# First cosine layer of a transformer tail: the first matrix product cut in halves of four token tiles, with the odd tile turned

## The chip, the core and the metric

The kernel runs on one core of a Trainium2 chip. The metric is the device time of one execution in microseconds, the median of several. Engines are named as the profile names them: PE (matmul), PEld (its weight loads), DVE (vector engine), ACT (scalar engine), POOL, and SP, which here only issues DMAs.

## What is computed

Random-feature attention, then a dense mixture of four experts, then a layer with a cosine. The reference, cut to what matters here:

```python
x = attn_out                                  # 1152 tokens x 512
out = sum(p[:, e] * (relu(x @ w1[e]) @ w2[e]) for e in range(4))   # w1 512 x 1024
h = out @ w_in                                # w_in 512 x 2048
g = h * np.cos(h)
return g @ w_out                              # w_out 2048 x 512
```

## The kernel before

The 2048 features of the cosine layer are done as two layers of 1024, so that six layers of one shape follow each other: e = 0 to 3 are the experts, e = 4 (E in the code) is the **first cosine layer**, e = 5 the **second cosine layer**. Tokens lie in nine tiles of 128. All matrix products are in float32r with each operand split into a high and a low part, so one product of blocks is three matmuls per 128 of depth.

**First product of a layer** (`first_product`, L552). The 1024 features are cut in four blocks p = 0 to 3 of two times 128. Tokens and weights of a block form a two by two scheme, which a Strassen-Winograd form does with seven products of six matmuls each: a, d, b, c, e are written to a fresh PSUM bank each, a2 is added onto the bank of a, and c2 onto the bank of c (`reopen`). After d, b, c, e and c2 DVE adds the bank into `h` (L571); after a ACT copies it. The token side uses sums T1 to T4 and the weight side sums S (the `load_a` chain: ACT splits at L129, DVE subtracts at L134 and forms sums at L184). c2 can't write its bank before DVE's add of c has read it.

In a layer that is `wide` the two token halves have four tiles (matmuls of 512 columns) and the ninth, the **odd tile**, is done apart by `odd_tile` (L522) with tokens as stationary operand and weights as moving one, so its result is turned and is turned back by eight transposes in the second product (L654). `together` says how many weight blocks one such matmul takes: two (512 columns), or one (256). Before, layers 1 to 3 and 5 are wide, `together` is two in 1 to 3 and one in 5. Layer 4 isn't wide: its halves have three tiles (384 columns), and the three tiles left over are done by `plain` (L509) with 24 matmuls of 384 columns per block.

**Second product** (`Second`, L632). Per token tile 24 matmuls of 512 columns (L704). Ahead of each half tile ACT and DVE split `h` into a high and a low part (`sth`, L674; `stl`, L677 or L282).

**Cosine** (`settle`, L386). A finished piece of `h` goes on `line`, and `from_line` (L429) takes one every `pace` quanta: ACT L400 and L401, DVE L403, ACT L408 (the sine), DVE L410 (the product). The scratch has three buffers. In layer 4 pieces of the last token chunk wait until the second product; in layer 5 pieces of the first token half wait until quantum 30.

**What sets the order.** A quantum is some six or twelve matmuls. `dense` (L839) runs the products, and after each quantum lets the pending helpers take one step; `plan` (L805) says after which quantum of which layer a helper starts. Engines are in order. Weight slots are handed on by `place` and `retired`: a weight load's split is issued once the slot's last reader is. Raw weights pass through two buffers (`new_raw`); the DMAs for them are issued by SP. The turned tokens of layer 4 come from the experts' sum `acc`: `second_x(1)` and `second_sums` in layer 3, `second_x(0)` for tiles 0 to 2 after quantum 2 of layer 4, since these three are the last of layer 3's order. The sums of the first column of tiles are made in layer 4's second product by `token_sums`, for layer 5.

Of the kernel before, what the change touches and what calls it, by code (L numbers as in the profile page):

```python
# [9 lines left out]
F32 = mybir.dt.float32  # L10
# [16 lines left out]
def performer_moe_kernel(ctx, tc, q, k, v, omega, probs, w1, w2, w_in, w_out, out):  # L27
# [59 lines left out]
    def wide(e, p):  # L87
        return 0 < e < E or e == E + 1

    def together(e):  # L90
        return 2 if e < E else 1
# [192 lines left out]
    def sum_out(n, src, cols):  # L284
        return split(nc.vector, src, *sums(n, cols))
# [38 lines left out]
    def token_sums(cols):  # L324
# [15 lines left out]
        ready.add(cols.start)  # L340
# [3 lines left out]
    def second_sums():  # L344

        cols = slice(1, HALF)
        r1, r2 = spare(cols)
        whole(r2, tokens(0, LO, cols))
        low = turn_acc(2, LO)
        yield  # L350
        for (_, tp), z in zip(low, range(J)):
            minus(r1[:, z], as_tiles(tp), r2[:, z])
        high = turn_acc(2, HI)
        yield
        put_second_x(2, high)
        parts = sum_out(1, r1, cols)
        next(parts)
        yield
        yield from parts
        for (_, tp), z in zip(high, range(J)):  # L360
            minus(r1[:, z], as_tiles(tp), r1[:, z])
        yield from wait(2)
        yield from rest_sums(r1, r2, cols)

# [64 lines left out]
    def from_line(q):  # L429

        since[0] += 1
        late_ = q >= FIRST[E]
        ready = sorted(
            (x for x in line if (x[3] > E and (x[0] == 2 or q >= 30)) or (x[3] == E and (x[0] < NCH - 1 or late_))),
            key=lambda x: (x[3], -x[0] if x[3] > E else x[0], *x[1:]),
        )
        pace = 2 if late_ or ready and ready[0][3] > E else 3
        if ready and ready[0][3] > E and ready[0][0] == 2 and ready[0][2] == NPF - 1:
            pace = 1
        if ready and since[0] >= pace:  # L440
            since[0] = 0
            line.remove(ready[0])
            c, i, p, e = ready[0]
            settled(e, c, i, p, None)
# [77 lines left out]
    def odd_tile(e, p):  # L522
# [14 lines left out]
        if together(e) > 1:  # L537
            retired.add(("a", e, p))
# [12 lines left out]

    def first_product(e):  # L552
        for p in range(NPF):
            o = not wide(e, p)
            cols = slice(o, HALF)
            W = (HALF - o) * P
            assert ready >= set(range(o, 2))
            a, s = unit("a", e, p), unit("s", e, p)
            A = {(i, j): (a, (i * KD + j * J) * P) for i in range(2) for j in range(2)}
            S = {n: (s, z * J * P) for n, z in ((1, 3), (2, 0), (3, 2), (4, 1))}  # L560
            b11, b21, b22 = (flat(tokens(*z, cols)) for z in ((0, LO), (0, HI), (1, HI)))
            t_ = {n: flat(sums(n, cols)) for n in (1, 2, 3, 4)}
            h = {(i, k): h_of(e, k + 1, i, p) for i in range(2) for k in range(2)}
            bk = {}

            def fresh(n, *args, W=W):
                bk[n] = bank(f"g1_{e}_{p}{n}")[:, :W]
                products(bk[n], *args)

            def add(dst, x, y):  # L570
                nc.vector.tensor_tensor(out=dst, in0=x, in1=y, op=ALU.add)  # L571

            def pa():
                fresh("a", *A[0, 0], b11)
                nc.scalar.activation(h[0, 0], bk["a"], ACTF.Copy)
                yield

            def pd():
                fresh("d", *S[2], t_[2])
                add(h[1, 0], bk["d"], h[0, 0])  # L580
                yield

            def pb():
                fresh("b", *S[1], t_[1])
                add(h[0, 1], bk["b"], h[1, 0])
                yield

            def pc():
                fresh("c", *S[3], t_[3])
                add(h[1, 1], bk["c"], h[0, 1])  # L590
                settle_later(e, 2, 1, p)
                yield

            def pe():
                fresh("e", *S[4], b22)
                add(h[0, 1], bk["e"], h[0, 1])
                settle_later(e, 2, 0, p)
                yield

            def pa2():  # L600
                products(bk["a"], *A[0, 1], b21, False, reopen=True)
                settle_later(e, 1, 0, p, bk["a"])
                yield

            def pc2():
                products(bk["c"], *A[1, 1], t_[4], False, reopen=True)
                add(h[1, 0], bk["c"], h[1, 0])
                settle_later(e, 1, 1, p)
                yield

            def rest(p):
                return [lambda: odd_tile(e, p + 1 - together(e))] * ((p + 1) % together(e) == 0) if wide(e, p) else [lambda i=i: plain(e, 0, i, p) for i in range(2)]

            z = rest(p)
            if e == 0:
                order = [pa, pd, pb, pc, pe, pa2, pc2]
            elif e == E and p == 0 or e == E - 1 and p == NPF - 1:
                order = [pa, pd, pb, pc, pe, pa2, pc2, *z]
            elif e == E and p == NPF - 1:
# [739 lines left out]
```

## Time and profile before

| | |
|---|---|
| Time, median of 3 runs | 656.94 us (656.5 to 657.05) |
| Profiled execution, its own time | 656.51 us |
| Its span | 654.6 us |
| PE busy | 649.9 us, 99% |
| DVE busy | 498.6 us, 76% |
| ACT busy | 362.7 us, 55% |
| POOL busy | 172.9 us, 26% |

The span runs from the first to the last instruction; 1.9 us of the profiled execution lie around it. A matmul record is longer than the distance to the next matmul, since matmuls are pipelined: distances between starts tell what a matmul costs. Layer 4's first product starts at 460.91 and its second at 508.02; layer 5's at 557.02 and 601.83.

### The profile page before, as it was taken

What the parts mean: (1) busy time and instruction counts of PE and PEld (TensorE: products, weight loads), DVE (VectorE), ACT (ScalarE), POOL (GpSimd) and SP (SyncE); (2) the same over time, 40 slices, a digit from 0 to 9 for tenths busy, and PEclk for the clock granted to TensorE, in tenths of its full rate; (3) what the DMA queues carried; (4) which work ended last, traced back from release to release, by engine and by line L of the source; (5) the groups of instructions that cost most, each with busy time, mean ns of one, the idle gap of its engine ahead of it and who ended that gap; (6) DMA issues with size and microseconds to landing.
All of it is one profiled execution on the core that took longest, in us unless ns stands there. A gap on an engine that the chain in (4) does not pass through costs nothing.

```text
span 654.6 us, 9478 instructions
## 1 busy us (share of the span) xinstructions
PE 649.9 (99%) x3407; PEld 568.7 (87%) x3407; DVE 498.6 (76%) x909; ACT 362.7 (55%) x719; POOL 172.9 (26%) x225
## 2 busy tenths in 40 slices
PE   9999999999999999999999999999999999999997
PEld 8999998998888888888888888888999888888887
DVE  6898749779879777679788588689688677596842
ACT  6887764446544545344544345554476874467821
POOL 8888461204332222333432322320000000000000
PEclk9999999999999999999999999999999999999999
DMA  8753121323344534345534245410810001700111
GB/s 190 217 160 98 34 65 33 97 64 114 136 156 140 199 111 142 117 133 171 181 115 145 106 162 176 145 65 4 318 34 32 1 1 50 273 1 1 49 49 49
DMA packets 55439, 70.93 MB, mean 108 GB/s; under 512 B 15200, under 2 KB 40032, under 8 KB 55392
## 3 DMA queue, kind: packets, MB, share of 16 engines
q1 hardware_dynamic: 46800, 40.92, 20.1%
q0 software_dynamic: 8448, 29.37, 12.9%
q8 instruction: 27, 0.44, 0.3%
q14 instruction: 20, 0.16, 0.1%
q10 hardware_dynamic: 144, 0.03, 0.0%
HBM read 55.36 MB, written 14.94 MB: 107 GB/s over the span
## 4 chain that ended last, share of the span: by engine, by line
PE 99%; DVE 0%; issue 0%
PE g L704 45%; PE g L503 5%; PE g_odd L533 3%; PE g_0a L503 2%; PE g_3a L503 2%; PE g_2c L503 2%; PE g_2a L503 2%; PE g_1a L503 2%; PE g_0c L503 2%; PE g_3c L503 2%; PE g_1c L503 2%; PE kv L1085 2%; PE num L1114 2%; PE pj_q L1005 2%; PE pj_k L1005 2%; PE g_3e L503 1%
## 5 line engine op out<-in xcount | busy, mean ns | idle before, releaser
L674 ACT ACTIVATE sth<-h 128x512 fp32r<-128x512 f32 (+1 forms) x114 | 61.5, 551 | 70.3 <-PE g L704 55.1
L248 POOL TENSOR_TENSOR c<-c 128x512 uint32<-128x512 uint32 x32 | 45.9, 1434 | 84.3 <-issue 26.6
L677 DVE SCALAR_TENSOR_TENSOR stl<-h,sth 128x512 fp32r<-128x512 f32 (+1 forms) x72 | 50.3, 715 | 22.7 <-ACT sth L674 22.3
L704 PE MATMUL g<-v3h,sth 128*128 128x512 f32 (+1 forms) x110 | 42.9, 390 | 0.0
L704 PE MATMUL g<-v1h,sth 128*128 128x512 f32 (+1 forms) x110 | 42.7, 388 | 0.0
L704 PE MATMUL g<-v0h,sth 128*128 128x512 f32 (+1 forms) x110 | 42.6, 387 | 0.0
L704 PE MATMUL g<-v2h,sth 128*128 128x512 f32 (+1 forms) x110 | 42.5, 386 | 0.0
L704 PE MATMUL g<-v0h,stl 128*128 128x512 f32 (+1 forms) x110 | 42.5, 386 | 0.0
L704 PE MATMUL g<-v3h,stl 128*128 128x512 f32 (+1 forms) x110 | 42.4, 386 | 0.0
L704 PE MATMUL g<-v1h,stl 128*128 128x512 f32 (+1 forms) x110 | 42.4, 386 | 0.0
L704 PE MATMUL g<-v0l,sth 128*128 128x512 f32 (+1 forms) x110 | 42.4, 386 | 0.0
L704 PE MATMUL g<-v2h,stl 128*128 128x512 f32 (+1 forms) x110 | 42.4, 385 | 0.0
L704 PE MATMUL g<-v1l,sth 128*128 128x512 f32 (+1 forms) x110 | 42.4, 385 | 0.0
L704 PE MATMUL g<-v3l,sth 128*128 128x512 f32 (+1 forms) x110 | 42.4, 385 | 0.0
L704 PE MATMUL g<-v2l,sth 128*128 128x512 f32 (+1 forms) x110 | 42.4, 385 | 0.0
L282 DVE TENSOR_TENSOR stl<-h,sth 128x512 fp32r<-128x512 f32 (+1 forms) x42 | 24.4, 588 | 21.1 <-ACT sth L674 20.8
L403 DVE SCALAR_TENSOR_TENSOR c<-c 128x384 f32<-128x384 f32 (+2 forms) x44 | 25.8, 591 | 9.0 <-ACT c L401 8.8
L233 ACT ACTIVATE c<-c 128x512 f32<-128x512 f32 x32 | 21.1, 658 | 10.6 <-DMA kv_0h<-c 5.5
L232 ACT ACTIVATE c<-c 128x512 f32<-128x512 uint32 x32 | 21.2, 663 | 10.2 <-DMA c<-in_moe_w_in_dram 7.7
L401 ACT ACTIVATE c<-c 128x384 f32<-128x384 f32 (+2 forms) x44 | 24.4, 555 | 1.4
L704 PEld LDWEIGHTS g<-v0h,stl 128*128 128x128 f32 x110 | 20.7, 188 | 4.4
L704 PEld LDWEIGHTS g<-v1h,stl 128*128 128x128 f32 x110 | 20.7, 188 | 4.2
(430 smaller groups left out, 2003.5 us busy)
## 6 DMA issues: line engine op xcount, KB each, us to landing
rv<-in_moe_w_dram SPq DMA_DIRECT2D x16, 512.0 KB, 3.8
c<-in_moe_w_in_dram POOLq DMA_DIRECT2D x16, 512.0 KB, 4.2
c<-in_moe_w_out_dram POOLq DMA_DIRECT2D x16, 512.0 KB, 3.9
kt<-in_k_dram SPq DMA_DIRECT2D x8, 256.0 KB, 3.6
qt<-in_q_dram SPq DMA_DIRECT2D x8, 256.0 KB, 3.5
ve<-in_v_dram SPq DMA_DIRECT2D x16, 128.0 KB, 2.9
ra_2as<-in_moe_w_dram SPq DMA_DIRECT2D x8, 256.0 KB, 3.1
ra_3as<-in_moe_w_dram SPq DMA_DIRECT2D x8, 256.0 KB, 3.1
```

Of the source, the lines that this page charges most:

```text
L232: nc.scalar.activation(lw.bitcast(F32), lw, ACTF.Copy, bias=2.0, scale=2.0**-51)
L233: nc.scalar.activation(t.bitcast(F32), hw.bitcast(F32), ACTF.Abs)
L248: nc.gpsimd.tensor_tensor(out=total, in0=t, in1=lw, op=ALU.add)
L282: nc.vector.tensor_tensor(out=dst, in0=x, in1=y, op=ALU.subtract)
L401: nc.scalar.activation(kk, vv, ACTF.Copy, bias=ROUND)
L403: nc.vector.scalar_tensor_tensor(out=vv, in0=kk, scalar=ROUND, in1=vv, op0=ALU.subtract, op1=ALU.subtract)
L503: nc.tensor.matmul(dst, x[:, o], y[:, kk], start=start and n == 0, stop=stop and n == 3 * kn - 1, skip_group_check=reopen,)
L533: nc.tensor.matmul(g, x[:, kk], w[:, :, :, kk, :], start=n == 0, stop=n == 3 * KD - 1)
L674: nc.scalar.activation(hi, src, ACTF.Relu if self.e < E else ACTF.Copy)
L677: nc.vector.scalar_tensor_tensor(out=to, in0=src, scalar=0.0, in1=hi.bitcast(F32), op0=ALU.max, op1=ALU.subtract)
L704: nc.tensor.matmul(g, x, y[:, o : o + w], start=n == 0, stop=n == 3 * FT - 1)
L1005: nc.tensor.matmul(pj[:, i * 256 : (i + 1) * 256], a[:, cs], b_, start=z == 0, stop=z == 2)
```

## The change

Layer 4 becomes wide, and `together` is two everywhere.

- Layer 4's first product has 42 matmuls of 512 columns per block and two odd products of twelve. Its second product starts with tile 2, the odd one, in the order that layer 5 has, and turns it with eight transposes.
- Products a and a2 of blocks 0 and 1 come first (`ahead`), then block 0's d, b, c, e, c2, then the odd product of blocks 0 and 1, then block 1's d, b, c, e, c2. Blocks 2 and 3 keep the order a, d, b, c, e, a2, c2, with the second odd product ahead of block 3.
- In layer 5 the odd product of blocks 0 and 1 comes ahead of block 1, that of blocks 2 and 3 ahead of block 3; before there was one per block.
- The tokens of tiles 0 and 1 and all sums for the first column of tiles are now made at the end of layer 3 (`tile_x(0)`, `tile_sums`), tile 2 after quantum 2 of layer 4. `token_sums` in layer 4's second product is gone. The scratch of `tile_sums` is one of the two raw weight buffers.
- The raw loads of blocks 2 and 3 of layer 4 start after quanta 2 and 6, not 6 and 17, as in every wide layer.
- Pieces of layer 4 no longer wait on `line`; those of the first token half have pace 3 before quantum 30.

```diff
     def wide(e, p):
-        return 0 < e < E or e == E + 1
+        return e > 0
 
     def together(e):
-        return 2 if e < E else 1
+        return 2
...
     def sum_out(n, src, cols):
-        return split(nc.vector, src, *sums(n, cols))
+        yield from split(nc.vector, src, *sums(n, cols))
+        ready.add((n, cols.start))
...
-    def second_sums():
-
-        cols = slice(1, HALF)
+    def second_sums(cols, turned, put_high):
+
+        ready.difference_update((n, cols.start) for n in (1, 2, 3, 4))
...
-        put_second_x(2, high)
+        low = turned(LO)
+        yield
+        for src, z in zip(low, range(J)):
+            minus(r1[:, z], src, r2[:, z])
+        high = turned(HI)
+        yield
+        put_high(high)
         parts = sum_out(1, r1, cols)
         next(parts)
         yield
         yield from parts
-        for (_, tp), z in zip(high, range(J)):
-            minus(r1[:, z], as_tiles(tp), r1[:, z])
-        yield from wait(2)
+        for src, z in zip(high, range(J)):
+            minus(r1[:, z], src, r1[:, z])
+        if cols.start:
+            yield from wait(2)
         yield from rest_sums(r1, r2, cols)
...
+    def turn_tile(t):
+        tp = as_tiles(bank(f"tx2_t{t}"))
+        for kk in range(KD):
+            nc.tensor.transpose(tp[:, kk, :], acc[t][:, kk * P : (kk + 1) * P], ident)
+        return tp
+
+    def put_tile(t, tp, ks):
+        xh, xl = (x[:, ks, pos[t], :] for x in x_t)
+        nc.scalar.activation(xh, tp[:, ks], ACTF.Copy)
+        minus(xl, tp[:, ks], xh.bitcast(F32))
+
+    def tile_x(t):
+
+        tp = turn_tile(t)
+        yield
+        put_tile(t, tp, slice(0, KD))
+
+    def tile_sums():
+
+        tp = turn_tile(1)
+        yield from second_sums(
+            slice(0, 1), lambda ks: [tp[:, kk : kk + 1, :] for kk in range(KD)[ks]], lambda _: put_tile(1, tp, HI)
+        )
 
...
     def from_line(q):
 
         since[0] += 1
-        late_ = q >= FIRST[E]
         ready = sorted(
-            (x for x in line if (x[3] > E and (x[0] == 2 or q >= 30)) or (x[3] == E and (x[0] < NCH - 1 or late_))),
-            key=lambda x: (x[3], -x[0] if x[3] > E else x[0], *x[1:]),
+            (x for x in line if x[3] == E or x[0] == 2 or q >= 30), key=lambda x: (x[3], -x[0], *x[1:])
         )
-        pace = 2 if late_ or ready and ready[0][3] > E else 3
-        if ready and ready[0][3] > E and ready[0][0] == 2 and ready[0][2] == NPF - 1:
+        pace = 2
+        if ready and ready[0][0] == 2 and ready[0][2] == NPF - 1:
             pace = 1
+        elif ready and ready[0][0] == 1 and q < 30:
+            pace = 3
         if ready and since[0] >= pace:
             since[0] = 0
             line.remove(ready[0])
...
-        if together(e) > 1:
-            retired.add(("a", e, p))
+        retired.update((("a", e, p), ("odd", e, p + 1)))
+        if ("block", e, p + 1) in retired:
+            retired.add(("a", e, p + 1))
...
+    def block(e, p):
+
+        o = not wide(e, p)
+        cols = slice(o, HALF)
+        W = (HALF - o) * P
+        early = e == E and p < 2
...
+        first = h[1, 0] if early else h[0, 0]
+
+        def pa():
+            fresh("a", *A[0, 0], b11)
+            nc.scalar.activation(first, bk["a"], ACTF.Copy)
+            yield
...
+        def pa2():
+            products(bk["a"], *A[0, 1], b21, False, reopen=True)
+            settle_later(e, 1, 0, p, bk["a"])
+            yield
+
+        def pc2():
+            retired.add(("s", e, p))
+            if not wide(e, p) or ("odd", e, p) in retired:
+                retired.add(("a", e, p))
+            retired.add(("block", e, p))
+            assert ready >= {(4, z) for z in range(o, 2)}
+            products(bk["c"], *A[1, 1], t_[4], False, reopen=True)
+            add(h[1, 0], bk["c"], h[1, 0])
+            settle_later(e, 1, 1, p)
+            yield
+
+        return pa, pa2, pd, pb, pc, pe, pc2
+
     def first_product(e):
+        ahead = [block(e, p) for p in range(2)] if e == E else []
+        for n in range(2):
+            for steps in ahead:
+                yield from steps[n]()
         for p in range(NPF):
...
-            def rest(p):
-                return [lambda: odd_tile(e, p + 1 - together(e))] * ((p + 1) % together(e) == 0) if wide(e, p) else [lambda i=i: plain(e, 0, i, p) for i in range(2)]
-
-            z = rest(p)
-            if e == 0:
-                order = [pa, pd, pb, pc, pe, pa2, pc2]
-            elif e == E and p == 0 or e == E - 1 and p == NPF - 1:
-                order = [pa, pd, pb, pc, pe, pa2, pc2, *z]
-            elif e == E and p == NPF - 1:
-                order = [pa, z[0], pd, pb, pc, z[1], pe, pa2, pc2]
-            elif e == E + 1 and p == NPF - 1 or together(e) > 1 and p == 1:
-                order = [*z, pa, pd, pb, pc, pe, pa2, pc2]
+            pa, pa2, *mid, pc2 = ahead[p] if p < len(ahead) else block(e, p)
+            z = [lambda: odd_tile(e, p - 1)] * (p % 2) if wide(e, p) else []
+            if p < len(ahead):
+                order = [*z, *mid, pc2]
+            elif e == E - 1 and p == NPF - 1:
+                order = [pa, *mid, pa2, pc2, *z]
+            elif e >= E and p == NPF - 1 or p == 1:
+                order = [*z, pa, *mid, pa2, pc2]
             else:
-                order = [pa, pd, pb, pc, pe, *z, pa2, pc2]
-            for n, step in enumerate(order):
-                if n == len(order) - 1:
-                    retired.add(("s", e, p))
-                    if not wide(e, p) or (p + 1) % together(e) == 0:
-                        retired.add(("a", e, p))
+                order = [pa, *mid, *z, pa2, pc2]
+            for step in order:
                 yield from step()
...
         start_at(E - 1, FIRST[E - 1] + 14, second_x, 1)
-        start_at(E - 1, FIRST[E - 1] + 25, second_sums)
-        start_at(E, 2, second_x, 0)
+        start_at(E - 1, FIRST[E - 1] + 25, chunk_sums)
+        start_at(E - 1, FIRST[E - 1] + 30, tile_x, 0)
+        start_at(E - 1, FIRST[E - 1] + 33, tile_sums)
+        start_at(E, 2, tile_x, 2)
         start_at(0, 70, token_sums, slice(0, 1))
-        start_at(E, FIRST[E] + 22, token_sums, slice(0, 1))
...
             elif e == E:
-                order = [*range(NTILE)]
+                order = [2, 6, 7, 8, 1, 0, 3, 4, 5]
```

The order on PE in layer 4, block 1, from the last half of product e on (g is the bank, w02 and w3 are weights, T4 a token sum). Before:

```order
L503 MATMUL g_4_1e<-xh,w3h 128x384
L503 MATMUL g_4_1e<-xl,w3h 128x384
L503 MATMUL g_4_1e<-xh,w3l 128x384
L503 MATMUL g_4_0_0_1_4705<-xh,w02h 128x384
L503 MATMUL g_4_0_0_1_4705<-xl,w02h 128x384
L503 MATMUL g_4_0_0_1_4705<-xh,w02l 128x384
```

After:

```order
L538 MATMUL g_4_1e<-xh,w3h 128x512
L538 MATMUL g_4_1e<-xl,w3h 128x512
L538 MATMUL g_4_1e<-xh,w3l 128x512
L538 MATMUL g_4_1c<-T4h,w02h 128x512
L538 MATMUL g_4_1c<-T4l,w02h 128x512
L538 MATMUL g_4_1c<-T4h,w02l 128x512
```

Before, the 24 plain matmuls and a2 stand between e and c2; now c2 (onto the bank g_4_1c) follows e at once.

The order on DVE in the same block, up to its add of c (c_97 is the cosine's scratch, ra_2as the raw weights of block 2, w02l a weight slot). Before:

```order
L403 SCALAR_TENSOR_TENSOR c_97<-c_97 128x384 x2
L410 TENSOR_TENSOR h<-g_4_0_0_0_4612,c_97 128x3x128
L571 TENSOR_TENSOR h<-g_4_1d,h 128x384
L410 TENSOR_TENSOR h<-h,c_97 128x384
L134 TENSOR_TENSOR w02l<-ra_2as,w02h 128x1024
L184 TENSOR_TENSOR ra_2as<-ra_2as 128x256 x2
L571 TENSOR_TENSOR h<-g_4_1b,h 128x384
L410 TENSOR_TENSOR h<-g_4_0_1_0_4631,c_97 128x3x128
L184 TENSOR_TENSOR ra_2as<-ra_2as 128x256 x2
L571 TENSOR_TENSOR h<-g_4_1c,h 128x384
L571 TENSOR_TENSOR h<-g_4_1e,h 128x384
```

After:

```order
L445 TENSOR_TENSOR h<-h,c_97 128x512
L438 SCALAR_TENSOR_TENSOR c_97<-c_97 128x512 x2
L610 TENSOR_TENSOR h<-g_4_1d,h 128x512
L445 TENSOR_TENSOR h<-h,c_97 128x512
L134 TENSOR_TENSOR w02l<-ra_2as,w02h 128x1024
L184 TENSOR_TENSOR ra_2as<-ra_2as 128x256 x2
L610 TENSOR_TENSOR h<-g_4_1b,h 128x512
L184 TENSOR_TENSOR ra_2as<-ra_2as 128x256 x2
L610 TENSOR_TENSOR h<-g_4_1c,h 128x512
L445 TENSOR_TENSOR h<-h,c_97 128x512
```

The add of c has much the same work ahead of it, but the pieces of the cosine are of 512 columns, and the second of the two L438 operations is that of the odd product.

The order on ACT from the last piece of the first product to the split of a later tile, in layer 4 (sth is the split, th the turned odd tile). Before:

```order
L421 ACTIVATE h<-g_4_3a 128x384
L408 ACTIVATE c_97<-c_97 128x384
L400 ACTIVATE c_97<-h 128x384
L401 ACTIVATE c_97<-c_97 128x384
L674 ACTIVATE sth<-h 128x512
L400 ACTIVATE c_97<-h 128x384
L401 ACTIVATE c_97<-c_97 128x384
L674 ACTIVATE sth<-h 128x512
```

After:

```order
L435 ACTIVATE c_97<-h 128x512
L436 ACTIVATE c_97<-c_97 128x512
L720 ACTIVATE sth<-th_0_4889 128x256 x2
L720 ACTIVATE sth<-th_1_4899 128x512
L456 ACTIVATE h<-g_4_3a 128x512
L443 ACTIVATE c_97<-c_97 128x512 x2
L435 ACTIVATE c_97<-h 128x512
L436 ACTIVATE c_97<-c_97 128x512
L443 ACTIVATE c_97<-c_97 128x512
L435 ACTIVATE c_97<-h 128x512
L436 ACTIVATE c_97<-c_97 128x512
L720 ACTIVATE sth<-h 128x512
```

Now the split of tile 6, the last row, stands behind three splits of the odd tile and three sines (L443); before, splits of whole tiles stood among the pieces.

## Rows read from the trace of the kernel before

**Rows 1.** Page, part 4: the chain that ended last, share by engine.

```profile
PE 99%; DVE 0%; issue 0%
```

**Rows 2.** Busy us (and count) by stretch: PE, PEld, DVE, ACT, POOL; clock, DMA, GB/s.

```profile
460.91:508.02 47.11, 47.11 (x277) 47.04 (x276) 35.86 (x67) 30.50 (x63) 0.00 (x0) 1.00 0.30 113
...
557.02:601.83 44.81, 44.81 (x225) 38.11 (x224) 32.36 (x54) 26.63 (x50) 0.00 (x0) 1.00 0.25 95
```

**Rows 3.** Timeline of PE: start, duration, engine, line, operation; products of both cosine layers.

```profile
473.70 0.33 PE L503 MATMUL g_1a<-xh,w02h 128*128 128x384 f32 x1
...
474.74 0.33 PE L503 MATMUL g_1d<-T2h,w3h 128*128 128x384 f32 x1
...
563.82 0.28 PE L533 MATMUL g_odd<-w02h,xh 128*128 128x256 f32 x1
...
565.25 0.40 PE L503 MATMUL g_0a<-xh,w02h 128*128 128x512 f32 x1
...
566.64 0.39 PE L503 MATMUL g_0c<-T4h,w02h 128*128 128x512 f32 x1
```

**Rows 4.** Timeline of PE at the end of layer 5's first product.

```profile
598.23 1.03 PE L654 MATMUL th<-ident,h 128*128 128x128 f32 x8
599.02 0.48 PE L503 MATMUL g_3a<-xh,w02h 128*128 128x512 f32 x1
...
600.47 0.39 PE L503 MATMUL g_3c<-T4h,w02h 128*128 128x512 f32 x1
...
601.83 0.39 PE L704 MATMUL g<-v0h,sth 128*128 128x512 f32 x1
```

**Rows 5.** Layer 4, block 1: PE at e and c2, DVE at c's add.

```profile
477.86 0.33 PE L503 MATMUL g_1e<-xh,w3h 128*128 128x384 f32 x1
...
484.10 0.33 PE L503 MATMUL g_1c<-T4h,w02h 128*128 128x384 f32 x1
...
482.59 0.55 DVE L571 TENSOR_TENSOR h<-g_1c,h 128x384 f32<-128x384 f32 x1
```

**Rows 6.** Layer 5, block 1: PE at e, DVE up to c's add.

```profile
573.44 0.39 PE L503 MATMUL g_1e<-xh,w3h 128*128 128x512 f32 x1
...
569.77 1.23 DVE L134 TENSOR_TENSOR w02l<-ra_2as,w02h 128x1024 fp32r<-128x1024 f32 x1
571.03 0.89 DVE L184 TENSOR_TENSOR ra_2as<-ra_2as 128x256 f32<-128x256 f32 x2
571.83 0.68 DVE L571 TENSOR_TENSOR h<-g_1d,h 128x512 f32<-128x512 f32 x1
572.43 0.68 DVE L410 TENSOR_TENSOR h<-h,c 128x512 f32<-128x512 f32 x1
...
574.62 0.69 DVE L571 TENSOR_TENSOR h<-g_1c,h 128x512 f32<-128x512 f32 x1
```

**Rows 7.** ACT in layer 5: cosine, weight split, and around the second product's start.

```profile
566.19 0.61 ACT L400 ACTIVATE c<-h 128x512 f32<-128x512 f32 x1
566.84 0.63 ACT L401 ACTIVATE c<-c 128x512 f32<-128x512 f32 x1
...
568.68 1.05 ACT L129 ACTIVATE w02h<-ra_2as 128x1024 fp32r<-128x1024 f32 x1
...
599.15 0.63 ACT L400 ACTIVATE c<-h 128x512 f32<-128x512 f32 x1
...
603.52 0.62 ACT L408 ACTIVATE c<-c 128x512 f32<-128x512 f32 x1
...
605.29 0.71 ACT L674 ACTIVATE sth<-h 128x256 fp32r<-128x256 f32 x2
```

**Rows 8.** DVE at the start of layer 4: the last sum of the other columns.

```profile
460.96 0.96 DVE L134 TENSOR_TENSOR T4l<-h,T4h 128x768 fp32r<-128x768 f32 x1
```

**Rows 9.** Timeline of SP: the issue of block 3's raw weights for layer 4.

```profile
459.40 0.39 SPq L164 DMA_DIRECT2D ra_3as<-ka_3a  x1
```

**Rows 10.** DMA issues: queue, count, KB each, median us to landing.

```profile
ra_3as<-ka_3a SPq DMA_DIRECT2D x2, 512.0 KB, 7.7
```

More of the change, by code (lines that the diff above doesn't have):

```diff
@@ L339, in token_sums @@
         yield from rest_sums(r1, r2, cols)
-        ready.add(cols.start)
     ready = set()
-    def second_sums():
-        cols = slice(1, HALF)
+    def second_sums(cols, turned, put_high):
+        ready.difference_update((n, cols.start) for n in (1, 2, 3, 4))
         r1, r2 = spare(cols)
         whole(r2, tokens(0, LO, cols))
-        low = turn_acc(2, LO)
+        low = turned(LO)
         yield
-        for (_, tp), z in zip(low, range(J)):
-            minus(r1[:, z], as_tiles(tp), r2[:, z])
-        high = turn_acc(2, HI)
+        for src, z in zip(low, range(J)):
+            minus(r1[:, z], src, r2[:, z])
+        high = turned(HI)
         yield
-        put_second_x(2, high)
+        put_high(high)
         parts = sum_out(1, r1, cols)
@@ L359, in second_sums, with chunk_sums, turned @@
         yield from parts
-        for (_, tp), z in zip(high, range(J)):
-            minus(r1[:, z], as_tiles(tp), r1[:, z])
-        yield from wait(2)
+        for src, z in zip(high, range(J)):
+            minus(r1[:, z], src, r1[:, z])
+        if cols.start:
+            yield from wait(2)
         yield from rest_sums(r1, r2, cols)
+    def chunk_sums():
+        tps = {}
+        def turned(ks):
+            tps[ks.start] = turn_acc(2, ks)
+            return [as_tiles(tp) for _, tp in tps[ks.start]]
+        yield from second_sums(slice(1, HALF), turned, lambda _: put_second_x(2, tps[HI.start]))
+    def turn_tile(t):
[16 more added lines that the diff above has]
+        )
     def advance(under):
@@ L550, in flat, with S, fresh, add @@
         return [x.rearrange("p k n f -> p k (n f)") for x in parts]
+    def block(e, p):
[3 more added lines that the diff above has]
+        early = e == E and p < 2
+        a = unit("a", e, p)
+        A = {(i, j): (a, (i * KD + j * J) * P) for i in range(2) for j in range(2)}
+        b11, b21, b22 = (flat(tokens(*z, cols)) for z in ((0, LO), (0, HI), (1, HI)))
+        t_ = {n: flat(sums(n, cols)) for n in (1, 2, 3, 4)}
+        h = {(i, k): h_of(e, k + 1, i, p) for i in range(2) for k in range(2)}
+        bk = {}
+        def S(n, t=True):
+            assert not t or ready >= {(n, z) for z in range(o, 2)}
+            return unit("s", e, p), {1: 3, 2: 0, 3: 2, 4: 1}[n] * J * P
+        def fresh(n, *args):
+            bk[n] = bank(f"g1_{e}_{p}{n}")[:, :W]
+            products(bk[n], *args)
+        def add(dst, x, y):
+            nc.vector.tensor_tensor(out=dst, in0=x, in1=y, op=ALU.add)
+        first = h[1, 0] if early else h[0, 0]
[3 more added lines that the diff above has]
+            yield
+        def pd():
+            fresh("d", *S(2), t_[2])
+            add(h[1, 0], bk["d"], first)
+            yield
+        def pb():
+            fresh("b", *S(1), t_[1])
+            add(h[0, 1], bk["b"], h[1, 0])
+            yield
+        def pc():
+            fresh("c", *S(3), t_[3])
+            add(h[1, 1], bk["c"], h[0, 1])
+            settle_later(e, 2, 1, p)
+            yield
+        def pe():
+            fresh("e", *S(4, False), b22)
+            add(h[0, 1], bk["e"], h[0, 1])
+            settle_later(e, 2, 0, p)
+            yield
+        def pa2():
+            products(bk["a"], *A[0, 1], b21, False, reopen=True)
+            settle_later(e, 1, 0, p, bk["a"])
+            yield
+        def pc2():
[7 more added lines that the diff above has]
+            settle_later(e, 1, 1, p)
+            yield
+        return pa, pa2, pd, pb, pc, pe, pc2
@@ L552, in first_product @@
     def first_product(e):
+        ahead = [block(e, p) for p in range(2)] if e == E else []
+        for n in range(2):
+            for steps in ahead:
+                yield from steps[n]()
         for p in range(NPF):
[L554 to L609, printed above, removed]
```

## The prediction

> **What bounds the kernel now.** I read the chain of waits first: PE holds 99% of it, and no other engine a whole per cent [rows 1]. Then the stretches: in the first product of both cosine layers PE is busy for the whole length, 47.11 of 47.11 us and 44.81 of 44.81, and POOL does nothing in either [rows 2]. So what an edit takes from PE's work is gained, if nothing new makes PE wait. DVE, with 35.86 busy of 47.11, is hidden now, and this cover is what I look at: what PE does between a product and the next use of what DVE makes of it. The sum is made against the profiled execution, 656.51 us; the median of the runs shown is 656.94, 0.43 higher.
>
> **PE's own work.** In layer 4 six matmuls of 384 columns take 1.04 us, 173.3 ns each [rows 3]; in layer 5 six of 512 take 1.36, 226.7 ns each [rows 4]. Removed are 4 blocks x (42 + 24) = 264 of the first, 45.76 us; added are 4 x 42 + 2 x 12 = 192 of the second, 43.52 us. That is -2.24. Layer 5's odd products: twelve matmuls of 256 take 1.43 us, and the six after them 1.39, not 1.36 [rows 3], so four groups cost 5.84; two groups of twelve at 512 cost 5.44. That is -0.40. The eight new transposes: in layer 5 such a group takes 0.79, and the six matmuls after it 1.45, not 1.36 [rows 4]: +0.88. The twelve transposes of tiles 0 to 2 stay twelve, in three groups where two were: +0.1. Together **-1.66 us**, if nothing waits.
>
> The rows give a matmul 13 ns over its columns at the full clock (226.7 against 213.3). The Trainium skill, "TensorE: Matmul & The Clock Gate", section "Back-to-back issue gap", gives 2.5 ns for an isolated one; by that rule wide matmuls would save less here, an estimated 1.46 us for the 2.24. The rows show otherwise, and I go by them.
>
> **Product c2 of block 1 in layer 4.** c2 may not write its bank before DVE's add of c has read it. Call cover what PE does between the end of c and c2, and lag the time from c's end to the add's end. Before, c ended at 477.86, the add at 482.59 + 0.55, so the lag is 5.28; c2 began at 484.10, so the cover is 6.24 and 0.96 are left [rows 5]. In layer 5 c ended at 573.44 and the add at 574.62 + 0.69: a lag of 1.87 [rows 6]. Now a2 has been moved ahead and the plain matmuls are gone: the cover is product e alone, 1.36. So the two lags seen bound the wait: 0.5 to 3.9 us. Between them I work out the chain by the new order. Let 0 be the end of the odd product, which is directly ahead of d, b, c, e, 5.44 us of PE. ACT begins the odd tile's cosine at about 0.2, as the last matmul's record outlasts its slot by 0.16; the first operation takes 0.65 to the next, the second 0.63 [rows 7], done at 1.5. Behind it in DVE's queue stand the cosine's rounding, the add of d and a cosine product at 0.60 each (571.83 to 572.43), the weight split w02l at 1.26, two weight sums at 0.80, the add of b at 0.60, two weight sums at 0.80, and the add of c at 0.69 [rows 6]. w02l needs ACT's split, 0.55 for a sine and 1.05 [rows 7] after 1.5, 3.1, in time for 3.3. The add ends at 1.52 + 3 x 0.60 + 1.26 + 0.80 + 0.60 + 0.80 + 0.69 = 7.47. PE could begin at 5.44: **+2.1 us**, near neither bound, and I take it.
>
> **Block 2 of layer 4.** From there DVE has no gap. Two cosine products, a rounding, the add of e (2.4 us) and the split w1l (1.23) [rows 6] follow the add of c, begun at 6.78, and w1l ends at 11.0; PE needs it for the third matmul of d, at 7.52 + 1.36 + 1.36 + 0.45 = 10.7: **+0.3**. Then the add of c2, a rounding, a product (1.8), w02l (1.26), two sums (0.80), the add of d, a rounding (1.2), two sums (0.80), the add of b, a product (1.2) and the add of c (0.69), 7.75 from 10.9, end at 18.7. PE has from 11.1 the rest of d (0.91) and b, c, e, a2 (5.44), and is at c2 at 17.4: **+1.3**. The three make 3.7; if the lags were those of layer 5, 0.5 to 1.
>
> Here each of DVE's operations begins 0.09 before the record ahead of it ends [rows 6]. The Trainium skill, "VectorE: DVE Perf Modes", section "The DRAIN you can't avoid", has the next one wait until the pipe is empty. If that meant a start behind the end of the record, the 28 operations of this chain would be an estimated 2.4 us longer and the time 663.6; the rows of distance show it isn't so, and it enters neither sum nor range.
>
> **Start of layer 4's second product.** In layer 5 the last piece of the cosine starts on ACT at 599.15 and the split of tile 6 at 605.29 [rows 7]; its second half ends at 606.00, and PE comes to tile 6 at 601.83 + 5.44 = 607.27 [rows 4]: 1.25 to spare. In layer 4 the new order puts one split (0.3) and one sine (0.55) more between the two, DVE's add of e is some 0.7 late by its full queue, and a piece that needs a scratch buffer waits for DVE's product behind three splits, some 1.2. The sum less 1.25 is 1.5; without the buffer's wait 0.3. I take **+1.4**, since pieces no longer wait on the line there.
>
> **Layer 5.** The cover of c2 shrinks from 4.18 (e, odd, a2) to 2.72 (e, a2). With the lag of before, 1.87 [rows 6], nothing is lost. By the chain from the odd product's end: ACT needs 0.2 + 0.65 + 0.63 + 0.55 + 1.05 = 3.1 up to the weight split [rows 7]; then w02l 1.26, two sums 0.80, an add 0.60, two sums 0.80, an add 0.60, the product of the odd tile, now 512 wide, 0.60, the add 0.69, ending at 8.4, against six products, 8.16: +0.3. Block 2 is alike without an odd product between, about +0.5. I take **+0.8**, with 0 as the other end.
>
> **What is hidden.** Token sums: DVE ended its last sum of the other columns at 461.9, 1.0 after layer 4's start [rows 8]; the layer now starts 0.9 later by two groups of transposes, and DVE has one operation of 0.60 more, so 0.7 after. Behind it stand nine operations of 128x256 or less at 0.40 and one eviction of 0.60 up to T2, which is there at 4.9; PE uses T2 after four products and a group of transposes, at 5.9. 1.0 is left; a microsecond more of DVE there is a microsecond of PE. Weights: SP issued block 3's raw load at 459.40 [rows 9], ahead of the layer; now it waits for the scratch of the sums, until about 10.5 us after the start, and the six loads for the second product's later weights queue behind it on SP. With 7.7 to landing [rows 10] it is there at 18; its split is due at about 27, and the six aren't used ahead of the second product, 38 us on. The sums removed from the second product lie beside PE's 216 matmuls and give nothing.
>
> **Sum.** -1.66 + 3.7 + 1.4 + 0.8 = +4.2: 660.7 for the profiled execution, **661.2 us** as the median.
>
> **Rivals.** *DVE keeps up.* If DVE's queue had its gaps elsewhere and each add came with layer 5's lag where the cover is 2.72 and within 1.36 in block 1, the work alone would decide: 656.94 - 1.66 = 655.3. For it speaks that DVE's busy share in both stretches is under 77% [rows 2]; against it that this is a mean, and that the lag of 5.28 in layer 4 shows a queue that is full just there [rows 5]. It decides from the point where the lag in block 1 is under 1.36. *Half of it.* If the lags in layer 4 are like layer 5's and the line is short at the second product, the waits are 0.5 to 3 and pay for the gain: 656 to 658. *The start is late too.* If the sums for the first column come 1 to 2 us late, everything behind shifts with DVE's queue: 662.5 to 663.5. For it speaks that only 1.0 is left there.
>
> **How the numbers follow.** My forecast, waits of 4 to 8 us in all, has 0.76; the late start 0.10; half of it 0.07; DVE keeps up 0.07. What a measurement can tell from no change is about 0.2%, 1.3 us. Faster has the 0.07 of the rival; same 0.07 from the half; slower 0.86. The range: low end, the first wait at its chain, the others at half, 2.1 + 0.8 + 0.3 - 1.66 = 1.5, so 658.5; high end, the sum with a late start of 2, 663.2.
>
> **What would show it.** In the changed kernel's trace PE would stand idle ahead of c2 of blocks 1 and 2 of layer 4, released by DVE's add of c; ahead of the third matmul of block 2's d, released by w1l; and at tile 6 of the second product, released by ACT's split. Layer 4's first product would take some 48.6 us, not 44.9 as without waits; the second 50.4, not 49.0. If PE has no gaps there and the first product is about 45 us long, the chain on DVE is wrong and the rival right. If the gap stands at block 0's d, the sums are late.

## The result, and the profile after

The changed kernel takes **661.80 us** (median of six runs, 661.48 to 662.70), the kernel before 656.99 beside it: a ratio of 1.0076, 95% interval 1.0063 to 1.0089. The forecast was 661.2, in a range from 658.5 to 663.2; the kernel became 0.8% slower, which is clear of the noise. The profiled execution took 661.48, its span is 659.5.

Page of the changed kernel, part 1 (busy us, share, count) and part 4 (chain that ended last):

```profile
PE 651.1 (99%) x3319; PEld 558.4 (85%) x3319; DVE 497.2 (75%) x892; ACT 360.8 (55%) x694; POOL 172.7 (26%) x225
...
PE 91%; DVE 5%; ACT 2%; issue 1%; DVEq 0%
```

PE's busy share reads 99% as before, but the chain that was PE alone [rows 1] now runs 5% over DVE and 2% over ACT. Stretches of the changed kernel, first product of layer 4 and of layer 5 (columns as in rows 2):

```profile
462.16:511.09 48.93, 46.03 (x205) 36.95 (x204) 42.08 (x74) 36.29 (x63) 0.00 (x0) 1.00 0.28 105
561.55:606.67 45.12, 45.02 (x201) 36.71 (x200) 31.77 (x50) 26.15 (x44) 0.00 (x0) 1.00 0.26 101
```

Against rows 2: PE was busy for all of 47.11 us, now for 46.03 of 48.93; DVE went from 35.86 to 42.08 in a stretch that is little longer. Lengths by stage, from the starts of the first matmuls, in us:

| | before | after | forecast |
|---|---|---|---|
| layer 3, second product | 52.68 | 53.61 | 53.6 |
| layer 4, first product | 47.11 | 48.93 | 48.6 |
| layer 4, second product | 49.00 | 50.45 | 50.4 |
| layer 5, first product | 44.81 | 45.13 | 45.2 |
| layer 5, second product | 52.78 | 52.78 | 52.8 |

Together +4.52; the profiled executions differ by 4.97, of which 0.32 lies ahead of these stages. Timeline of PE in the changed kernel at the places where it stands still; in brackets the idle time and its releaser:

```profile
464.65 0.39 PE L538 MATMUL g_1a<-xh,w02l 128*128 128x512 f32 x1
464.95 0.50 PE L538 MATMUL g_0a<-xh,w02h 128*128 128x512 f32 x1
465.28 0.39 PE L538 MATMUL g_0a<-xl,w02h 128*128 128x512 f32 x1
...
483.00 0.39 PE L538 MATMUL g_1e<-xh,w3l 128*128 128x512 f32 x1
485.27 0.50 PE L538 MATMUL g_1c<-T4h,w02h 128*128 128x512 f32 x1 [1.89 <-DVE h L610]
485.61 0.40 PE L538 MATMUL g_1c<-T4l,w02h 128*128 128x512 f32 x1
...
488.39 0.39 PE L538 MATMUL g_2d<-T2l,w1h 128*128 128x512 f32 x1
488.80 0.50 PE L538 MATMUL g_2d<-T2h,w1l 128*128 128x512 f32 x1
...
495.08 0.39 PE L538 MATMUL g_2a<-xh,w02l 128*128 128x512 f32 x1
496.45 0.50 PE L538 MATMUL g_2c<-T4h,w02h 128*128 128x512 f32 x1 [0.99 <-DVE h L610]
...
516.33 0.39 PE L750 MATMUL g<-v3h,stl 128*128 128x512 f32 x1
517.62 0.50 PE L750 MATMUL g<-v0h,sth 128*128 128x512 f32 x1 [0.90 <-ACT sth L720]
...
581.72 0.39 PE L538 MATMUL g_1a<-xh,w02l 128*128 128x512 f32 x1
582.14 0.50 PE L538 MATMUL g_1c<-T4h,w02h 128*128 128x512 f32 x1
```

A wait is read from starts, as 0.227 is the distance of two such matmuls: 483.00 to 485.27 is 2.27, so 2.05 were waited. The idle time in brackets is smaller, since it counts from the modelled end of the record ahead. Short waits, as at 488.39 to 488.80 (0.41), show no bracket at all and are found by distances alone.

### The profile page after: what moved, and what is told of

Read it like the earlier page. It is cut to its first block, busy times and chain, and to the rows that moved or that the text cites. A ratio compares the mean times of both kernels' runs of the same rounds, so it can differ in the third digit from the quotient of the medians.

```text
span 659.5 us, 9260 instructions
## 1 busy us (share of the span) xinstructions
PE 651.1 (99%) x3319; PEld 558.4 (85%) x3319; DVE 497.2 (75%) x892; ACT 360.8 (55%) x694; POOL 172.7 (26%) x225
## 4 chain that ended last, share of the span: by engine, by line
PE 91%; DVE 5%; ACT 2%; issue 1%; DVEq 0%
PE g L750 44%; PE g_odd L568 4%; PE g L538 3%; PE g_0a L538 2%; PE g_0c L538 2%; PE kv L1132 2%; PE num L1161 2%; PE g_2c L538 2%; PE g_1a L538 2%; PE g_3a L538 2%; DVE h L610 2%; PE g_3c L538 2%; PE pj_q L1052 2%; PE pj_k L1052 2%; PE g_2a L538 2%; PE g_1c L538 2%
## 5 line engine op out<-in xcount | busy, mean ns | idle before, releaser
L720 ACT ACTIVATE sth<-h 128x512 fp32r<-128x512 f32 (+1 forms) x111 | 60.1, 553 | 74.0 <-PE g L750 60.9
L282 DVE TENSOR_TENSOR stl<-h,sth 128x512 fp32r<-128x512 f32 (+1 forms) x39 | 22.8, 594 | 29.0 <-ACT sth L720 28.9
L438 DVE SCALAR_TENSOR_TENSOR c<-c 128x512 f32<-128x512 f32 x36 | 24.7, 687 | 8.9 <-ACT c L436 8.9
L435 ACT ACTIVATE c<-h 128x512 f32<-128x512 f32 x32 | 20.0, 626 | 15.7 <-DVE h L610 14.4
L750 PEld LDWEIGHTS g<-v0h,sth 128*128 128x128 f32 x110 | 20.7, 188 | 5.2 <-ACT sth L720 1.3
```

The lines of the kernel that those rows point to most:

```text
L282: nc.vector.tensor_tensor(out=dst, in0=x, in1=y, op=ALU.subtract)
L435: nc.scalar.activation(vv, src, ACTF.Copy, bias=0.25, scale=INV_2PI)
L438: nc.vector.scalar_tensor_tensor(out=vv, in0=kk, scalar=ROUND, in1=vv, op0=ALU.subtract, op1=ALU.subtract)
L720: nc.scalar.activation(hi, src, ACTF.Relu if self.e < E else ACTF.Copy)
L750: nc.tensor.matmul(g, x, y[:, o : o + w], start=n == 0, stop=n == 3 * FT - 1)
```

## The experiments

What the profiles compare best are the lengths of stages: the start of layer 3's second product, ahead of which no kernel here changes anything, lies between 408.2 and 410.1 in them. Where no ratio is given, the time is that of a single execution. Ratios and intervals are those of all executions on record, and differ a little from the ratio of the medians.

**Layer 5's odd products in pairs, alone** (in the kernel before):

```diff
-        return 2 if e < E else 1
+        return 2 if e != E else 1
```

> The kernel before with one part of the change alone: in layer 5 the odd product takes two weight blocks per matmul. Theory A (c2 waits when DVE's add of c lags by more than PE's cover): PE's work falls by 0.4 us, but c2 of blocks 1 and 2 of layer 5 waits about 0.2 each and restarts slowly (0.13 each), so layer 5's first product takes 45.1 us, not 44.8, and the time is 657.3. Rival W (only PE's work counts): 44.4 us without a gap, 656.6.

Measured: 657.36 against 657.81, ratio 0.9996 (0.9987 to 1.0005): no difference. Layer 5's first product takes 45.13, as in the changed kernel, for 44.81 before; c2 of block 1 starts 0.42 behind the matmul ahead of it, c2 of block 2 0.46. So the pairing doesn't give its 0.40 but takes 0.3, by waits at the two places that the forecast named; as a time this is too small to see.

**The changed kernel without early pieces**: the first token half's pieces of layer 4 wait for quantum 30, as layer 5's do.

```diff
-            (x for x in line if x[3] == E or x[0] == 2 or q >= 30), key=lambda x: (x[3], -x[0], *x[1:])
+            (x for x in line if x[0] == 2 or q >= 30), key=lambda x: (x[3], -x[0], *x[1:])
```

> The changed kernel, but pieces of layer 4's first token half wait on the line until quantum 30, as layer 5's do. Theory A: the wait at c2 of block 1 stays near 2.0 us (the pieces ahead of it are of the second half and of the odd tile), that at c2 of block 2 falls from 1.15 to some 0.3, since two or three pieces of 0.6 us leave DVE's queue, and the waits at tile 6 (1.4 with the slow restarts) go: 659.4. Rival C (the shortened cover alone makes the waits, whatever DVE has queued): the same 661.8.

Measured: 659.51, ratio 1.0032 (1.0020 to 1.0045), 2.3 us under the changed kernel's median (2.9 by the two ratios). The waits at c2 of block 2 and at tile 6 are gone (second product 48.96), c2 of block 1 waits its 2.05 as ever. So the pieces of the cosine, not the turning of the odd tile, make the wait at tile 6 and not the first one. For c2 of block 2 this profile alone doesn't show it, since PE itself was late there: the first product would be 1.3 shorter without that wait, and yet takes 48.92. The reason stands on PE. Its timeline in this kernel:

```profile
485.95 0.50 PE L538 MATMUL g_1c<-T4h,w02h 128*128 128x512 f32 x1 [1.89 <-DVE h L610]
...
487.56 0.63 PE L538 MATMUL g_2a<-xh,w02h 128*128 128x512 f32 x1
487.99 0.63 PE L538 MATMUL g_2a<-xl,w02h 128*128 128x512 f32 x1
```

The stretch from 487.20 of the same kernel (columns as in rows 2, the clock third from the end):

```profile
487.20:490.60 3.40, 3.40 (x10) 2.60 (x9) 3.08 (x5) 3.32 (x6) 0.00 (x0) 0.52 0.10 17
```

The matmuls are 0.43 apart, not 0.227, for seven distances (487.56 to 490.55): 512 columns at 1.2 GHz, the lower of the clock's two levels, at a granted clock of 0.52. With the slower distances on either side this cost 1.6 us. The changed kernel's profile has the same wait and kept a clock of 1.00. Three of the five executions show a mean clock of 0.997 (659.51, 659.71 and the profiled 660.61) and two one of 1.000 (659.02 and 659.26), so some executions have this loss and others don't. Of the changed kernel's six one shows 0.997, and at 661.64 it isn't longer than the others.

The late PE also hides DVE: the add of c of block 2 ended at 496.08, PE came to c2 at 497.25, 1.17 later. Without the 1.6 an estimated 0.2 to 0.5 of this wait would be left, as the expectation had it.

**c2 of block 1 behind a of block 2** (in the changed kernel), so that its cover is 2.72:

```diff
+            if e == E and p == 1:
+                held = order.pop()
+            elif e == E and p == 2:
+                order.insert(1, held)
```

> The changed kernel with c2 of block 1 moved behind product a of block 2, so that its cover is 2.72 us, not 1.36. Rival C (the place of c2): the wait shrinks by 1.36, 660.4. Theory A in its strong form (DVE's queue as a whole is late there): c2 waits only some 0.7, but d of block 2 then waits some 1.7 for the weight split w1l, which stands behind the same adds, and the time is 661.8 to 662.4.

Measured: 662.04, ratio 1.0068 (1.0054 to 1.0082). Timeline of PE:

```profile
484.20 0.39 PE L538 MATMUL g_2a<-xh,w02l 128*128 128x512 f32 x1
485.12 0.50 PE L538 MATMUL g_1c<-T4h,w02h 128*128 128x512 f32 x1 [0.53 <-DVE h L610]
...
486.84 0.39 PE L538 MATMUL g_2d<-T2l,w1h 128*128 128x512 f32 x1
488.64 0.50 PE L538 MATMUL g_2d<-T2h,w1l 128*128 128x512 f32 x1 [1.42 <-DVE w1l L134]
```

c2 now waits 0.69 for 2.05, but the third matmul of d 1.58 for 0.19 and c2 of block 2 1.63 for 1.15; the first product takes 49.44, 0.51 more than in the changed kernel, and the time can't be told from the changed kernel's. Cover at one place doesn't help: DVE's queue is behind as a whole, and the next thing PE needs of it is as late.

**No weight sums** for blocks 2 and 3 of layer 4, in the changed kernel; those weights stay unsummed, so this part of the computation is left out:

```diff
-        op(a22, a21, a22, ALU.add)
...
+        if e == E and p > 1:
+            yield
+        else:
...
```

> The changed kernel with the four weight sums on DVE left out for blocks 2 and 3 of layer 4 (the weight side of the scheme is left unsummed there). Theory A: 1.6 us less stands ahead of the add of c of block 1 in DVE's queue, so c2 of block 1 waits some 0.5 to 0.7, not 2.05, c2 of block 2 not at all; the waits at tile 6 stay: about 659.0. Rival P (ACT's cosine chain sets the time of the add, DVE's other work fits beside it): the waits change by under 0.3 each, 661.5.

Measured: 659.07; the first product takes 46.16, 2.77 less, c2 of block 1 starts 0.76 behind e's last matmul (a wait of 0.53), c2 of block 2 waits for nothing, the third matmul of d 0.23; tile 6 waits as before. Timeline of PE:

```profile
483.26 0.39 PE L541 MATMUL g_1e<-xh,w3l 128*128 128x512 f32 x1
484.02 0.50 PE L541 MATMUL g_1c<-T4h,w02h 128*128 128x512 f32 x1 [0.37 <-DVE h L613]
```

1.6 us off DVE's queue bring c2 forward by 1.51. This is the test of the cause: the queue ahead of the add of c, not the bank or PE, sets the wait.

**Without the odd tile's cosine in layer 4**, which is left out of the computation:

```diff
-        if e < E:
+        if e < E or e == E and i is None:
```

> The changed kernel without the cosine of the odd tile in layer 4: its products are copied out unchanged, so that the cosine of one tile of nine in that layer is left out. This takes ACT's three and DVE's two operations for each of two odd products off the line, and leaves weights and sums as they are. Theory A: the odd tile's rounding and product stand in DVE's queue ahead of the add of c, 0.6 us of the 2.05, and c2 of block 1 waits 1.4 to 1.7; c2 of block 2 waits as before, 1.1 to 1.3; with one piece fewer on the line tile 6 waits 0.5 or less; time about 660.1. Rival T (turning the odd tile itself, its copy and its transposes on PE, makes the waits): nothing changes, 661.5 or more.

Measured: c2 of block 1 starts 1.74 behind (a wait of 1.51, 0.53 less), tile 6 only 0.26 (0.03). Both are as expected; c2 of block 2 waits 0.91, a little under the 1.1 to 1.3 expected. Timeline of PE:

```profile
484.51 0.39 PE L538 MATMUL g_1e<-xh,w3l 128*128 128x512 f32 x1
486.25 0.50 PE L538 MATMUL g_1c<-T4h,w02h 128*128 128x512 f32 x1 [1.35 <-DVE h L610]
```

Its time, 661.42, isn't the expected 660.1: the five stages are 1.48 shorter than those of the changed kernel, but this execution came to them 1.52 later. They hold a new wait of 0.63, at the transposes of the odd tile (501.91), for ACT's copy of it. So the rounding of the odd tile is 0.53 of the 2.05. With the four sums' 1.51 that is as long as the wait; the last kernel below takes both out of this stretch of the queue.

**The sums on POOL**, which does nothing in these stretches: in the changed kernel, in the kernel before as a control, and together with the held pieces.

```diff
+        eng2 = nc.gpsimd if e >= E and p > 1 else eng
...
-            eng.tensor_tensor(out=dst, in0=x, in1=y, op=o)
+            eng2.tensor_tensor(out=dst, in0=x, in1=y, op=o)
```

> The changed kernel with the weight sums of blocks 2 and 3 of layers 4 and 5 on POOL instead of DVE, and nothing else. All of the work is done, unlike in e4_nosums. Theory A: as e4_nosums, c2 of block 1 waits 0.5 to 0.7, d of block 2 up to 0.8, c2 of block 2 hardly, tile 6 still 1.1 to 1.4; time 658.7 to 659.4, ratio 1.002 to 1.004. Rival Q (POOL's sums late, or DVE slowed beside them): waits of 2 us stay or new ones at weights appear, 661 or more.

> The kernel before with the same weight sums on POOL instead of DVE: a control for e5_hold_pool and e6_pool. Theory A: PE doesn't wait for DVE there, so 1.6 us less on DVE per block give nothing: 656.9, ratio 0.9990 to 1.0005. Rival Q: the sums on POOL come late or slow DVE, and this kernel is slower, 1.001 or more.

> Both causes taken away at once: pieces of the cosine of layer 4's first token half wait until quantum 30 (as in e2_hold), and the weight sums of blocks 2 and 3 of layers 4 and 5 are made by POOL, which does nothing there, instead of DVE. Theory A (DVE's queue ahead of the add of c makes PE wait, and the four sums are 1.6 us of it): the wait at c2 of block 1 falls from 2.05 to about 0.3 to 0.5, the waits at c2 of block 2, at tile 6 and in layer 5 are gone, and the time is some 0.7 us under the kernel before, ratio 0.9985 to 0.9995. Rival Q (work on POOL isn't free for DVE: a sum of 128x256 there takes up to 0.73 us against 0.40, comes late for the block after, or slows DVE's own operations beside it): PE waits at a weight of block 2 or 3, or DVE's records grow in these stretches, and the time is over the kernel before, 658 or more. Rival H (half-rate matmuls behind the wait, as in e2_hold): some 1.6 us more wherever a wait of over a microsecond is left.

Measured: the changed kernel with the sums on POOL takes 660.13, ratio 1.0051 (1.0037 to 1.0065), the control 657.12, 1.0001 (0.9992 to 1.0011), and the one with both 656.79, 0.9999 (0.9991 to 1.0008). The control's first products take 47.11 and 44.81, as without the edit: DVE's sums cost the kernel before nothing there. (Its second product of layer 4 is 0.35 longer, with a wait at 512.23 whose cause stays open.) The first came out 0.7 above the end of its expected range. Timeline of POOL in it:

```profile
482.31 3.88 POOL L185 TENSOR_TENSOR ra_2as<-ra_2as 128x256 f32<-128x256 f32 x4 [42.34 <-DMA v3h<-kv_3h]
```

Timeline of PE in it:

```profile
487.34 0.50 PE L539 MATMUL g_2d<-T2h,w1h 128*128 128x512 f32 x1 [0.63 <-ACT w1h L129]
487.67 0.40 PE L539 MATMUL g_2d<-T2l,w1h 128*128 128x512 f32 x1
488.60 0.50 PE L539 MATMUL g_2d<-T2h,w1l 128*128 128x512 f32 x1 [0.53 <-DVE w1l L134]
...
510.08 0.50 PE L751 MATMUL g<-v0h,sth 128*128 128x512 f32 x1 [0.30 <-ACT sth L721]
```

c2 of block 1 waits 0.53, as without sums, but four sums take 3.88 on POOL, 0.97 each for 0.40 on DVE, and the split behind them makes d wait 0.79 for w1h and 0.70 for w1l. That is rival Q of the expectation, in part. The last row is a wait that nobody expected, 0.46 at the start of the second product, for ACT's split of the odd tile; that product takes 50.94, 0.49 more than in the changed kernel. With the held pieces too, layer 5's first product takes 44.41, the 44.81 of before less the whole 0.40, and layer 4's second 48.96, but its first 46.53: 0.50 at c2 and 0.67 at w1l are left.

**The odd tile's cosine later as well**: to the kernel with both, a start of the odd product's cosine three quanta later.

```diff
-        settled(e, 0, None, p, g)
+        if e == E and p == 0:
+            settling.append(later_odd(e, p, g))
+        else:
+            settled(e, 0, None, p, g)
...
+    def later_odd(e, p, g):
+
+        yield from wait(3)
+        yield from settle(e, 0, None, p, g)
```

> e5_hold_pool with one thing more: in layer 4 the cosine of the first odd product starts three quanta later, behind product c of block 1, so that ACT makes block 2's weight split first and DVE's rounding of the odd tile stands behind the add of c. Theory A (what stands in DVE's queue ahead of the add of c decides): c2 of block 1 waits 0 to 0.2, not 0.50; d of block 2 still waits about 0.5 to 0.8 for w1l, because POOL's four sums of 0.88 lie in series ahead of its split. Time 0.4 to 0.6 under e5_hold_pool and the kernel before, ratio 0.9985 to 0.9997. Rival B (the bank of the odd product, held longer, makes a later product wait, or the weight split itself comes no earlier since it waits for the odd product on PE): c2's wait stays at 0.3 or more, or a new wait appears at a fresh bank, ratio 1.000 or more.

Measured: 656.57 against 656.93, ratio 0.9993 (0.9984 to 1.0002): it lies in the expected range, but can't be told from the kernel before. Timeline of DVE in it:

```profile
481.67 0.85 DVE L446 TENSOR_TENSOR h<-h,c 128x512 f32<-128x512 f32 x1
482.45 0.68 DVE L619 TENSOR_TENSOR h<-g_1c,h 128x512 f32<-128x512 f32 x1
```

POOL, beside it:

```profile
481.24 4.05 POOL L185 TENSOR_TENSOR ra_2as<-ra_2as 128x256 f32<-128x256 f32 x4 [41.35 <-DVE w02l L134]
```

ACT, whose split waits for POOL:

```profile
485.33 1.06 ACT L129 ACTIVATE w1h<-ra_2as 128x1024 fp32r<-128x1024 f32 x1 [0.87 <-POOL ra_2as L185]
```

PE, which waits for the split:

```profile
485.79 0.39 PE L539 MATMUL g_2a<-xh,w02l 128*128 128x512 f32 x1
486.44 0.50 PE L539 MATMUL g_2d<-T2h,w1h 128*128 128x512 f32 x1 [0.26 <-ACT w1h L129]
486.78 0.40 PE L539 MATMUL g_2d<-T2l,w1h 128*128 128x512 f32 x1
487.70 0.50 PE L539 MATMUL g_2d<-T2h,w1l 128*128 128x512 f32 x1 [0.53 <-DVE w1l L134]
```

The add of c begins at 482.45, and c2 waits for nothing, as theory A had it. But the first product takes 46.53 again: what c2 no longer waits, d now waits for w1h, since POOL's sums end at 485.29. The expected gain of 0.4 to 0.6 went there: the five stages are 0.07 under those of the kernel before, and were 0.08 under without this edit. No version beat the kernel before by more than can be measured.

## Why the prediction was right, point by point

**PE's own work, -1.66.** Where most waits are gone, in the kernel with both, the five stages are together 0.08 under those of before. Its waits are 0.50 and 0.67, the 0.07 at a2 (below), and 0.11 behind each of the three: 1.57. So the work alone is -1.65. The rows' 13 ns over the columns held, not the gap of the Trainium skill ("TensorE: Matmul & The Clock Gate", "Back-to-back issue gap"), by which it would have been smaller.

**c2 of block 1, +2.1.** DVE in the changed kernel, timeline; the last three rows are from later places:

```profile
479.28 0.69 DVE L438 SCALAR_TENSOR_TENSOR c<-c 128x512 f32<-128x512 f32 x1 [0.47 <-ACT c L436]
479.89 0.68 DVE L610 TENSOR_TENSOR h<-g_1d,h 128x512 f32<-128x512 f32 x1
480.49 0.68 DVE L445 TENSOR_TENSOR h<-h,c 128x512 f32<-128x512 f32 x1
481.09 1.22 DVE L134 TENSOR_TENSOR w02l<-ra_2as,w02h 128x1024 fp32r<-128x1024 f32 x1
482.34 0.89 DVE L184 TENSOR_TENSOR ra_2as<-ra_2as 128x256 f32<-128x256 f32 x2
483.14 0.68 DVE L610 TENSOR_TENSOR h<-g_1b,h 128x512 f32<-128x512 f32 x1
483.74 0.87 DVE L184 TENSOR_TENSOR ra_2as<-ra_2as 128x256 f32<-128x256 f32 x2
484.54 0.68 DVE L610 TENSOR_TENSOR h<-g_1c,h 128x512 f32<-128x512 f32 x1
...
487.54 1.21 DVE L134 TENSOR_TENSOR w1l<-ra_2as,w1h 128x1024 fp32r<-128x1024 f32 x1
...
495.72 0.68 DVE L610 TENSOR_TENSOR h<-g_2c,h 128x512 f32<-128x512 f32 x1
...
581.40 0.68 DVE L610 TENSOR_TENSOR h<-g_1c,h 128x512 f32<-128x512 f32 x1
```

The odd product ended at 477.79, where d's first matmul starts. The chain put the add of c 6.78 behind that, at 484.57; it began at 484.54, and PE went on at 485.27, 0.05 behind the record's end. The first eight rows are the chain, operation by operation in the order that the forecast had them in. The bounds, 0.5 and 3.9, were far apart, and the choice between them was right because the queue was written out by the order instead of scaled from a lag. The adds and products here start 0.60 apart with records of 0.68, so these operations overlap. Not each does, as the prediction says: behind w02l the next began 0.03 after the record's end, in [rows 6] and here (482.34), which the chain's 1.26 for it allowed for. The rule in "VectorE: DVE Perf Modes", "The DRAIN you can't avoid", of the Trainium skill would, read as the prediction reads it, have made this chain longer; the section adds that a next operation that isn't held starts earlier, and with that the rows agree.

**Block 2 of layer 4, +0.3 and +1.3.** d waits 0.19 for w1l, c2 1.15 for the add of c (495.72 to 496.40), each with 0.11 behind it: 0.29 and 1.26.

**Tile 6, +1.4.** 1.06, and 0.38 in the three distances behind it (0.11, 0.16 where PE waits for the low part `stl`, and 0.11): 1.44. Timeline of ACT in the changed kernel:

```profile
514.05 0.63 ACT L435 ACTIVATE c<-h 128x512 f32<-128x512 f32 x1 [1.20 <-DVE h L445]
...
515.77 0.62 ACT L435 ACTIVATE c<-h 128x512 f32<-128x512 f32 x1
516.42 0.63 ACT L436 ACTIVATE c<-c 128x512 f32<-128x512 f32 x1
516.96 0.61 ACT L720 ACTIVATE sth<-h 128x512 fp32r<-128x512 f32 x1
```

ACT stands still for 1.20 until DVE's product frees a scratch buffer, and the split of tile 6 ends at 517.57, while PE needed it at 516.56. The buffer was the term on which the forecast chose between 0.3 and 1.5, and it is there.

**Layer 5, +0.8.** c2 of blocks 1 and 2 wait 0.19 and 0.23, with 0.11 each: 0.64. In block 1 the add began at 581.40 and ended at 582.08, and c2 began at 582.14: with its restart 0.30, as the chain had it. Block 2 was put at 0.5 without a chain written out, and came to 0.34: the one term that is too large even with the restart counted in.

**Hidden.** T2's low part ended at 466.37, PE used it at 468.27: 1.9 left, not 1.0, so that the late start didn't happen. SP issued block 3's raw load at 472.24, 10.1 behind the layer's start; the forecast had 10.5, and nobody waited for it.

**What was missed.** a2 of block 0, moved ahead, adds onto the bank that ACT copies for a (0.59 at 464.30, to 464.89), and starts 0.07 late, with 0.11 behind it: 0.18. The 0.11 behind each wait was in no term. Measured are 2.16 + 0.29 + 1.26 + 1.44 + 0.64 + 0.18 = 5.97 of waits, forecast 5.9. That these two agree so closely is in part luck: the waits proper are 5.10, 0.8 less than the forecast had, and the slow restarts, which were in none of its terms, add 0.87. 5.97 less the stages' 4.52 leaves -1.45 for PE's work in this execution, 0.2 short of the -1.65 above. Most of that lies in matmuls behind the restarts that are 0.230 to 0.240 apart (485.61, 485.85, 486.09): from layer 4's start on, such distances come to 0.3 over 0.227 in the changed kernel, 0.16 more than in the kernel with both.

The rival *DVE keeps up* fell with the first gap; *half of it* fell with the lag of block 1, which is 3.35 (from 481.87, where e starts, to 485.22), not layer 5's 1.87 of before. *The start is late too* had 1.9 us in hand.

## What to carry to other kernels

Work taken off the bounding engine may have been the cover under which another engine kept up: before removing it, count what that other engine has queued ahead of the result that the bounding engine asks for next, operation by operation in the order of its queue, since a busy share of 76% says nothing of that place. If the queue is behind as a whole, moving the waiting instruction only moves the wait; taking operations off that stretch of the queue (here by holding the cosine's pieces and giving sums to an idle engine) is what shortens it, and the slower engine's own chain is then the next to look at.

## What the runs showed of the hardware

- The matmul of 512 columns behind a wait is slow: the next starts 0.335 to 0.340 later, not 0.227, at all eight waits of the changed kernel (485.27 to 485.61), and 0.333 to 0.343 at those of the experiments. A wait costs 0.11 more than its length, even one of 0.03 (tile 6 without the odd tile's cosine, 0.337).
- A wait of 2.05 us was followed in one profile by a fall of the granted clock to 0.52, 1.3 us after PE had gone on, which seven matmuls show (0.427 apart, 487.56 to 490.55), and in another, with the same wait at the same place, by no fall.
- A sum of 128x256 on POOL took 0.72 to 0.74 us in 47 of the 64 made there by the four kernels with sums on POOL, 41 of them beside other operations of DVE. In the 16 at whose start DVE was in an operation of two SBUF operands (a product like 481.67 in the last kernel, or the cosine's rounding) it took 0.93 to 1.13, longer by the overlap less 0.14: 0.19 for an overlap of 0.34, 0.33 for 0.47. The one left, 1.28, lies beside two roundings. Likewise the product, 0.68 alone, was 0.85 where it began 0.3 before a sum ended, while the add out of PSUM next to it kept its 0.68. The Trainium skill, "SBUF — State Buffer", section "Who interferes with whom", has a DVE instruction with two SBUF inputs contend with a GpSimd instruction that reads SBUF, and the page's "Summary: rules for kernel authors" has the second of the two wait until the first is done. The rows agree: what comes second is longer the more is left of the first.
